# Moving the routing pieces of a sparse-attention and expert kernel ahead of the masks within a step, and releasing its last value loads

## The chip, the cores and the metric

The kernel runs on one core of a Trainium2 chip. The metric is the time of one execution in device microseconds (us). Several executions of each kernel are timed and their median is compared. One further execution is recorded by the hardware profiler; every row below is from that one.

## The reference

Attention over 8 batches and 8 heads of 576 positions with 64 columns, then a layer of experts over the 4608 rows that result. Heads 0 to 3 look at the last 32 positions ("local"), heads 4 to 7 at every 32nd position ("strided").

```python
stride = 32
scores = scale * np.matmul(q, k.transpose(0, 1, 3, 2))
mask_local = (rel >= 0) & (rel < stride)
mask_strided = (rel >= 0) & (pos[None, :] % stride == pos[:, None] % stride)
masks = np.stack([mask_local if h < H // 2 else mask_strided for h in range(H)], axis=0)
scores = np.where(masks[None, :, :, :], scores, -1000000000.0)
attn = np.exp(scores - np.max(scores, axis=-1, keepdims=True))
attn = attn / (np.sum(attn, axis=-1, keepdims=True) + 1e-09)
x = np.matmul(attn, v)                      # then rows (batch, position) of 512 columns
logits = x @ w_gate + modality_bias[modality_id]
e_idx = np.argmax(logits, axis=1)           # one expert of 8 for each row
for e in range(E):
    mask = e_idx == e
    h = np.maximum(x[mask] @ w1[e], 0.0)    # 512 -> 1024
    out[mask] = gate_w[mask, None] * (h @ w2[e])
```

## The kernel before, in words

The work has two stages. The attention stage (about the first 147 us) goes over 32 units, `units`, which alternate between the classes `Local` and `Strided`. Eight units in a row belong to one pair of batches, so there are four pairs, `bp` 0 to 3; unit numbers 7, 15, 23 and 31 end a pair (`ends`). The expert stage then takes 12 blocks of rows, one after the other, each through the two matrices of its expert, in `ffn`.

The attention stage is one loop over steps, `for n in range(nu + 3)`. Several units are in flight in a step. In step n TensorE issues, in the order of the text (`manual_schedule` holds TensorE to it):

1. the scores of unit n (`scores`, L354 for a local unit, L449 for a strided one);
2. in some steps a piece of routing that was flagged as early (`waited`, `pop(1)`);
3. the transposes of the exponents of unit n-2 (`turn`, L224, tiles `t` or `ts`), whose result ScalarE and VectorE copy out (`et` at L378 and L381, `eb` at L484 and L488);
4. the masks of unit n+1 (`masks`, L343 or L442), which open the tiles that its scores are added to;
5. the values of unit n-3 (`values`, L391 and L397, or L499);
6. at the end of the step, transposes of a finished part of the pair (`turn_rows`, tile `xs`, copied at L514) in the two steps behind the end of a pair, and one piece of the work that a finished pair leaves (`pop(1)`).

That work is the generator `after`, which runs `finish_pair` and `route`. For pairs 0 to 2 its pieces come one a step, from step 8bp+10 on: transposes of the rows (tile `xl`, copied at L524), the logits (`lg`, L597 and L602, copied at L605), their transposes (`lt`) with transposes `xs`, more `xs`, the ranks (`rk`, L663 and L664, which read the running counts that L645 writes), and the entries of the lookup table (`en`, L695). The early piece of item 2 is `en`.

All tiles that TensorE writes come from one pool of eight banks of PSUM (`pa`), so a bank has to be emptied by ScalarE or VectorE before it is written again. On the engines other than TensorE a planner orders the instructions that aren't pinned, and it also picks the bank.

Loads are issued from SyncE's queue (SP), in the order of the text. Queries and keys come three steps ahead (`load`, L316 and L419). Values come in two parts each (`load_values`, L324 for a local unit, L424 for a strided one): part 0 of unit n-1 is issued in step n and is held by `after_landing` until TensorE has done the last transpose of unit n-2 (`point`), and part 1 until it has done the last value matmul of unit n-3 (`valued`). Local units take two buffers of `vv` in turn, strided ones two of `vsp`. Stores of finished rows (`store_rows`, L585 on SP for pair 2) stand behind them in the same queue, in the order of the text. From step 27 (`BEGIN`) each step also issues two gathers for the expert stage on GpSimd's queue (POOL); each waits for the last evacuation of the values in front of it (`pace`).

Of the kernel before, what the change touches and what calls it, by code (L numbers as in the profile page):

```python
# [40 lines left out]
SETUP = 6  # L41
POPS, POPF = 5, 3
LT, RS, RK = 7, 9, 11
LAG = 2
PLANE, SEND, SPLIT, TURN = 1, 3, 6, 4
LAST, DRAIN = 6, 4
WHEN = {1: 0, 3: 1, 5: 2, 7: 3}
# [1 line left out]
EARLY, BEGIN, HOLD = 3, 27, 26  # L49
# [142 lines left out]
def attention_moe(ctx: ExitStack, tc: tile.TileContext, a, out):  # L192
# [7 lines left out]
    def pa(name):  # L200
        return ps.tile([P, 512], F32, tag="a", name=name)
# [7 lines left out]
    def keep_busy(n, name):  # L209
        t = pa(name)  # L210
        for _ in range(n):
            nc.tensor.matmul(t, idle[:, 0:P], idle[:], start=True, stop=True)  # L212
# [10 lines left out]
    def turned_to(dst, src):  # L223
        return nc.tensor.transpose(dst, src, ident)  # L224
# [14 lines left out]
    def routing_setup():  # L239

        pin(nc.sync.dma_start(rt[:], a["rt"]))
        pin(nc.sync.dma_start(ld[0:1, :], a["nul"][:, 0:2]))
        pin(nc.sync.dma_start(xd[NT:NT + 1, :].bitcast(I32), a["nul"][:, 2:2 + DM]))
        modf = lp.tile([P, 36], F32, bufs=1, name="modf")
        pin(nc.gpsimd.tensor_copy(modf[:], modi))
        nmod = lp.tile([P, 36], F32, bufs=1, name="nmod")
        pin(nc.gpsimd.tensor_scalar(nmod[:], modf[:], -1.0, 1.0, ALU.mult, ALU.add))
        bias0 = lp.tile([P, 36, E], F32, bufs=1, name="bias0")

        def bc_e(t):  # L250
            return t.unsqueeze(2).to_broadcast([P, 36, E])

        def bc_t(t):
            return t.unsqueeze(1).to_broadcast([P, 36, E])

        pin(nc.gpsimd.tensor_tensor(bias[:], bc_e(modf), bc_t(mb[:, 1, :]), ALU.mult))
        pin(nc.gpsimd.tensor_tensor(bias0[:], bc_e(nmod), bc_t(mb[:, 0, :]), ALU.mult))
        pin(nc.gpsimd.tensor_tensor(bias[:], bias[:], bias0[:], ALU.add))
# [46 lines left out]
    class Local:  # L305
# [62 lines left out]
        def turn(self):  # L368
            n, ex = self.n, self.ex
            self.et = et = ets[0]  # L370
            t1 = pa(f"t1{n}").rearrange("p (g q) -> p g q", g=4)
            for k in range(4):
                turned_to(t1[:, k, :], ex[:, 2 * k:2 * k + 2, :])
            t2 = pa(f"t2{n}")[:, :P]
            self.point = turned_to(t2, ex[:, 9:11, :])
            for par in range(2):
                r = slice(64 * par, 64 * par + 64)
                nc.scalar.copy(et[r, 0:16, par, :], t1[r].rearrange("p k (u q) -> p (k u) q", u=4))  # L378
            for jj in range(2):
                r = slice(64 * jj, 64 * jj + 64)  # L380
                nc.scalar.copy(et[r, 16:18, jj, :], t2[r, 64 * jj:64 * jj + 64].rearrange("p (b q) -> p b q", b=2))  # L381
# [127 lines left out]
    def turn_rows(bp, xt, xcs, c, k0):  # L509
        kn = min(4, 9 - k0)  # L510
        t = pa(f"xs{bp}{c}{k0}").rearrange("p (g q) -> p g q", g=4)
        for k in range(kn):
            turned_to(t[:, k, :], xcs[2 + c][:, P * (k0 + k):P * (k0 + k + 1)])
        nc.scalar.copy(xt[:, k0:k0 + kn, 256 + P * c:256 + P * c + P], t[:, :kn, :])  # L514
# [64 lines left out]
    stores, tabulating = [], []  # L579
# [281 lines left out]
    def after_landing(ins, other):  # L861
        tc.add_manual_dep(ins.ins, other.ins.name, landed, reason="transfers kept apart")
# [90 lines left out]
    def settle(n):  # L953
        while len(late) > n:
            late.pop(0)()
# [55 lines left out]
    def ffn(fp, n, xh, xl, les, between, load=None):  # L1011
# [40 lines left out]
        for f in range(8):  # L1052
# [12 lines left out]
            between(f)  # L1065
            settle(LAG)
        if wide:
# [11 lines left out]
    units, ends = [], {}  # L1079
# [10 lines left out]
    def after(bp, xt, xcs):  # L1090
        yield from finish_pair(bp, xt, xcs)
        if bp >= EARLY:
            yield
            yield from tabulate(bp)
# [10 lines left out]
    def pop(k):  # L1105
        for _ in range(k):
            early.clear()
            while extra:
                got = next(extra[0], extra)
                if got is not extra:  # L1110
                    early.extend([got] if got else ())
                    break
                extra.pop(0)
# [43 lines left out]
    def issue(count):  # L1157
        for _ in range(count):
            if queue and (queue[0][0] >= len(plan) or plan[queue[0][0]][1] in tables):
                queue.pop(0)[1]()  # L1160
# [6 lines left out]
    for what in ORDER.split():  # L1167
        i = int(what[1])
        queue.append((0, partial(load, 0, i)) if what[0] == "w" else (i, partial(begin[what[0]], i)))

    nu = len(units)
# [12 lines left out]
    for n in range(nu + 3):  # L1184
        if n + 3 < nu:
            units[n + 3].load(0)
        if n in FILL:
            keep_busy(FILL[n], f"warm{n}")
        if n < nu:
            units[n].scores()  # L1190
        waited = bool(early)
        if n + 3 < nu:
            after_landing(units[n + 3].load(1), units[n].scored)
        if waited:
            pop(1)
        if 2 <= n <= nu + 1:
            units[n - 2].turn()
        if 1 <= n <= nu:
            ins = units[n - 1].load_values(0)
            if n >= 2:  # L1200
                after_landing(ins, units[n - 2].point)
        if n + 1 < nu:
            units[n + 1].masks()
        if n == nu + 1:
            turn(0)
        if n >= 3:
            units[n - 3].values()
        if 1 <= n <= nu:
            ins = units[n - 1].load_values(1)
            if ins and n >= 3:  # L1210
                after_landing(ins, units[n - 3].valued)
        if n >= 3:
            if n - 3 in ends:
                extra.append(after(*ends[n - 3]))
        if n == SETUP:
            routing_setup()
        if n + 2 < nu:
            units[n + 2].prep()
        ready = len(stores) if n >= HOLD else 9
        if n - 1 in ends or n - 2 in ends:  # L1220
            turn_rows(*ends[n - 1 if n - 1 in ends else n - 2], 0 if n - 1 in ends else 1, 0)
        pop(POPS if n == nu + 2 else 1)
        for _ in range(min(ready, STORED.get(n, SPREAD[(n - 2) % 8]))):
            if stores:
                stores.pop(0)()
        if n >= BEGIN:
            issue(2)
        if n in TABLES:
            for _ in tabulating[-1]:
                break  # L1230
# [6 lines left out]
    for k, (n, *_) in enumerate(plan):  # L1237
        def between(f):
            pop(POPF)
            if TURNED <= k + 1 < len(plan):  # L1240
                if f == PLANE:
                    sent[k + 1] = plane_tokens(plan[k + 1][0], *gathered[k + 1])
                if f == SEND:
                    sent[k + 1] = send_tokens(*sent[k + 1])
                if f == SPLIT:
                    turned[k + 1] = split_tokens(plan[k + 1][0], (k + 1) % 2, *sent[k + 1])
            elif f == TURN:
                turn(k + 1)
            if k + 1 == width and f == LAST:
                turned[width] = turn_last(*gathered[len(plan)], turned[width])  # L1250
            if k == width and f == DRAIN:
                pin(nc.gpsimd.drain())
            issue((2, 1, 1, 1, 2, 1, 2, 1)[f] if k == 0 else f > 1)
# [60 lines left out]
```

## Time and profile before

| | |
|---|---|
| median of 3 runs | 583.21 us |
| lowest and highest of them | 580.5 and 588.86 us |
| the profiled execution | 581.83 us |
| its span, first to last instruction | 580.0 us |
| TensorE busy (modelled ends) | 564.3 us, 97% of the span |
| VectorE, ScalarE, GpSimd busy | 381.7, 325.0 and 197.2 us |

The span lies inside the time of its execution, here 1.83 us shorter. "Busy" is the time in which an engine has an instruction running; a matmul's end is modelled, so TensorE's idle time is read from the list of its waits and from the times between groups. "Issue" as a releaser means that the profile shows nothing that the engine waited for. In the chain of work a group's time is the time until its successor, without the modelled tail.

### The profile page before, as it was taken

The numbers are of one execution on the slowest core, as the hardware profiler recorded it, in microseconds if no ns is written. First come the engines' busy times: TensorE is split into PE (matmuls) and PEld (weight loads), VectorE is DVE, ScalarE is ACT, GpSimd is POOL, SyncE is SP. The second block draws the span as 40 slices with busy tenths as digits, with TensorE's granted clock in tenths as the row PEclk, the third lists the DMA queues.
The fourth block names the chain that finished last, engine by engine and source line by source line (L and its number), as shares of the span: only waits on it lengthen the run. The fifth ranks groups of instructions, "written<-read, shape, count | busy, mean of one in ns | idle before, by whom it ended". The sixth has DMA issues, their size and how long they took to land.

```text
span 580.0 us, 13584 instructions
## 1 busy us (share of the span) xinstructions
PE 564.3 (97%) x5383; PEld 495.1 (85%) x5385; DVE 381.7 (66%) x909; ACT 325.0 (56%) x646; POOL 197.2 (34%) x198
## 2 busy tenths in 40 slices
PE   9999999998999999999999999999999999999995
PEld 5878888877788899989999998989898998998884
DVE  7886977967867874676674757666475666655410
ACT  5789898897744544554454544545363555545312
POOL 3011120125464315444344334554434445320102
PEclk9999999999999999999999999999999999999999
DMA  8988898978985308566543266142414156772102
GB/s 299 332 287 298 287 326 292 327 229 296 313 296 196 118 12 308 187 199 223 154 164 74 61 211 216 47 88 73 90 33 99 52 200 174 262 162 72 56 0 76
DMA packets 62699, 104.28 MB, mean 180 GB/s; under 512 B 36451, under 2 KB 36963, under 8 KB 58532
## 3 DMA queue, kind: packets, MB, share of 16 engines
q0 software_dynamic: 15456, 57.47, 28.6%
q1 hardware_dynamic: 45636, 43.29, 25.5%
q10 hardware_dynamic: 1536, 2.58, 1.4%
q8 instruction: 44, 0.72, 0.5%
q14 instruction: 27, 0.22, 0.1%
HBM read 94.09 MB, written 19.18 MB: 195 GB/s over the span
## 4 chain that ended last, share of the span: by engine, by line
PE 82%; issue 10%; ACT 3%; DVE 2%; POOL 1%; POOLq 0%; ACTq 0%
PE h L1022 31%; PE o L1037 30%; PE s L354 3%; PE ss L449 3%; PE o L391 2%; PE ot L499 2%; PE lg L597 2%; PE xl L224 2%; PE t L224 2%; PE xs L224 1%; PE warm L212 1%; PE ts L224 1%; POOL out L1044 1%; ACT xc L507 1%; PE en L695 1%
## 5 line engine op out<-in xcount | busy, mean ns | idle before, releaser
L1059 DVE TENSOR_TENSOR wl<-raw,wh 128x512 fp32r<-128x512 f32 x176 | 115.2, 692 | 66.8 <-ACT wh L1058 56.7
L1058 ACT CAST wh<-raw 128x512 fp32r<-128x512 f32 x176 | 100.5, 619 | 99.4 <-PE o L1037 81.5
L1022 PE MATMUL h<-xh,wl 128*128 128x384 f32 x352 | 118.7, 337 | 0.0
L1022 PE MATMUL h<-xl,wh 128*128 128x384 f32 x352 | 118.2, 336 | 0.0
L1022 PE MATMUL h<-xh,wh 128*128 128x384 f32 x352 | 117.4, 337 | 0.0
L1037 PE MATMUL o<-wl,hh 128*128 128x512 f32 x264 | 104.1, 394 | 0.0
L1037 PE MATMUL o<-wh,hl 128*128 128x512 f32 x264 | 104.0, 395 | 0.0
L1037 PE MATMUL o<-wh,hh 128*128 128x512 f32 x264 | 103.2, 391 | 0.0
L1025 ACT ACTIVATE hh<-h 128x384 fp32r<-128x384 f32 x88 | 43.2, 491 | 82.4 <-PE h L1022 71.0
L1027 DVE SCALAR_TENSOR_TENSOR hl<-h,hh 128x384 fp32r<-128x384 f32 x88 | 48.9, 555 | 56.5 <-ACT hh L1025 55.1
L921 POOL DMA_INDIRECT raw<-in_w,wi x44 | 51.8, 1177 | 61.3 <-ACT hh L1025 50.8
L1022 PEld LDWEIGHTS h<-xh,wh 128*128 128x128 f32 x352 | 66.2, 188 | 4.2 <-PE xs L224 0.4
L1022 PEld LDWEIGHTS h<-xl,wh 128*128 128x128 f32 x352 | 66.1, 188 | 2.9
L1022 PEld LDWEIGHTS h<-xh,wl 128*128 128x128 f32 x352 | 66.0, 188 | 0.4 <-DVE wl L1059 0.4
L889 POOL DMA_INDIRECT fx<-xd,le x33 | 37.2, 1129 | 76.8 <-ACT wh L1058 42.2
L1037 PEld LDWEIGHTS o<-wh,hl 128*128 128x128 f32 x264 | 49.5, 188 | 10.5
L1037 PEld LDWEIGHTS o<-wl,hh 128*128 128x128 f32 x264 | 49.5, 188 | 8.6
L1037 PEld LDWEIGHTS o<-wh,hh 128*128 128x128 f32 x264 | 49.6, 188 | 8.2
L906 POOL DMA_INDIRECT le<-ld,li x33 | 35.5, 1076 | 41.9 <-DVE li L828 17.6
L1044 POOL DMA_INDIRECT out<-y,le x33 | 34.6, 1049 | 41.3 <-ACT y L1043 37.0
L589 POOL DMA_DIRECT2D xd<-xt x18 | 10.0, 558 | 64.9 <-ACT xc L507 28.2
L983 DVE COPY work<-fx 128x1536 uint16<-128x1536 uint16 x16 | 27.2, 1743 | 0.0
(215 smaller groups left out, 872.6 us busy)
## 6 DMA issues: line engine op xcount, KB each, us to landing
vv<-in_vl SPq DMA_DIRECT2D x32, 292.5 KB
qks<-in_qks SPq DMA_DIRECT2D x32, 288.0 KB
qk<-in_qkl SPq DMA_DIRECT2D x16, 304.0 KB
qk<-in_qkl SPq DMA_DIRECT2D x16, 288.0 KB
xd<-xt POOLq DMA_DIRECT2D x18, 256.0 KB
vsp<-in_vs SPq DMA_DIRECT2D x16, 256.0 KB
xd<-xt SPq DMA_DIRECT2D x9, 256.0 KB
xd<-xt ACTq DMA_DIRECT2D x2, 1024.0 KB
```

What stands on the lines that cost most here:

```text
L224: return nc.tensor.transpose(dst, src, ident)
L889: ins = in_turn(nc.gpsimd.indirect_dma_start(xt[:, h, :], None, xd[0:xrows, :], IOA(ap=le[:, h, 0:1], axis=0), **bounds))
L906: in_turn(nc.gpsimd.indirect_dma_start(le[:, h, :], None, ld[0:1 + last, :], IOA(ap=li[:, s, h:h + 1], axis=0)))
L921: ins = nc.gpsimd.indirect_dma_start(raws[j].rearrange("p f c -> p (f c)"), None, a["w"], IOA(ap=wi[:, s, j:j + 1], axis=0), bounds_check= ...
L983: pin(nc.vector.tensor_copy(rows[:, :, w, :], halves(xt)[:, :, :, w]))
L1022: nc.tensor.matmul(hp, w[:, a1], x[:, c, 0:size], start=(k == 0), stop=(k == 11))
L1025: steps.append(nc.scalar.activation(hh[:, 0:size], hp, AF.Relu))
L1027: nc.vector.scalar_tensor_tensor(hl[:, 0:size], hp, 0.0, hh[:, 0:size].bitcast(F32), ALU.max, ALU.subtract)
L1037: nc.tensor.matmul(os[h], hx[:, m], w[:, 512:1024], start=(f == 0 and i == 0), stop=(f == 7 and i == 2))
L1044: outs.add(in_turn(nc.gpsimd.indirect_dma_start(out, IOA(ap=le[:, i, 0:1], axis=0), y[:], None, bounds_check=NT - 1, oob_is_err=False), True))
L1058: nc.scalar.copy(wh[:, c], raw[:, c])
L1059: nc.vector.tensor_tensor(wl[:, c], raw[:, c], wh[:, c].bitcast(F32), ALU.subtract)
```

## The change

It has two parts. First, `turn_rows` and the pair's piece `pop(1)` no longer stand at the end of a step but right behind `turn` of unit n-2, in front of the value load, the masks and the values. In the step in which a pair's generator is appended (n-3 in `ends`) and in the last step, the piece stays at the end. Second, the value loads of units 28 to 31 are no longer held by `after_landing`; unit 28's are issued in step 29 as before, those of units 29 and 30 both in step 30, and unit 31's in step 31, so units 30 and 31 come a step sooner in the text.

```diff
-LAG = 2
+LAG, FREE = 2, 29
...
         if 2 <= n <= nu + 1:
             units[n - 2].turn()
-        if 1 <= n <= nu:
+        ready = len(stores) if n >= HOLD else 9
+        if n - 1 in ends or n - 2 in ends:
+            turn_rows(*ends[n - 1 if n - 1 in ends else n - 2], 0 if n - 1 in ends else 1, 0)
+        beside = n <= nu + 1 and n - 3 not in ends
+        if beside:
+            pop(1)
+        if 1 <= n < FREE:
             ins = units[n - 1].load_values(0)
             if n >= 2:
                 after_landing(ins, units[n - 2].point)
+        for i in {FREE: (FREE - 1,), FREE + 1: (FREE, FREE + 1), FREE + 2: (FREE + 2,)}.get(n, ()):
+            for part in range(2):
+                units[i].load_values(part)
         if n + 1 < nu:
             units[n + 1].masks()
         if n == nu + 1:
             turn(0)
         if n >= 3:
             units[n - 3].values()
-        if 1 <= n <= nu:
+        if 1 <= n < FREE:
             ins = units[n - 1].load_values(1)
             if ins and n >= 3:
                 after_landing(ins, units[n - 3].valued)
...
-        ready = len(stores) if n >= HOLD else 9
-        if n - 1 in ends or n - 2 in ends:
-            turn_rows(*ends[n - 1 if n - 1 in ends else n - 2], 0 if n - 1 in ends else 1, 0)
-        pop(POPS if n == nu + 2 else 1)
+        if not beside:
+            pop(POPS if n == nu + 2 else 1)
         for _ in range(min(ready, STORED.get(n, SPREAD[(n - 2) % 8]))):
```

## Rows read from the trace of the kernel before

**Rows 1.** Windows: length, busy PE, PEld, DVE, ACT, POOL; clock, DMA share, GB/s.

```profile
0.00:120.00 120.00, 114.78 (x2697) 95.85 (x2700) 98.72 (x354) 99.79 (x226) 18.84 (x37) 1.00 0.91 304
120.00:147.00 27.00, 23.14 (x473) 18.93 (x474) 18.49 (x69) 22.25 (x54) 12.78 (x13) 1.00 0.80 272
147.00:573.00 426.00, 426.00 (x2216) 380.30 (x2215) 264.52 (x487) 202.28 (x367) 163.62 (x147) 1.00 0.45 140
```

**Rows 2.** Waits of PE, 0 to 165 us: total, times, longest.

```profile
PE s L354 <- issue: 2.2, 2, 1.1
PE ss L449 <- issue: 1.2, 2, 0.9
PE o L391 <- issue: 1.2, 3, 0.4
...
PE o L391 <- ACT xt L514: 0.6, 2, 0.3
PE ts L224 <- DVE pbf L676: 0.6, 1, 0.6
PE ot L499 <- ACT eb L488: 0.6, 1, 0.6
```

**Rows 3.** Chain of work, step 20: start, time, what.

```profile
85.10 1.15 PE ot L499 x32
86.25 1.86 PE lg L597 x32
```

**Rows 4.** Timeline of PE, step 15: start, time, instruction, idle before and releaser.

```profile
63.33 0.41 PE L343 MATMUL s<-cb_sb 128*128 128x256 bf16 x2
...
64.79 0.69 PE L391 MATMUL o<-vv,et 128*64 128x65 f32 x16 [0.32 <-ACT xt L514]
```

**Rows 5.** Timeline of all engines, lines of ACT, steps 14 and 15.

```profile
59.59 1.18 ACT L378 COPY et<-t 64x512 f32<-64x512 f32 x2 [0.88 <-PE t L224]
...
64.17 0.73 ACT L514 COPY xt<-xs 128x512 f32<-128x512 f32 x2
```

**Rows 6.** Timeline of ACT, step 19: the copies of the row transposes.

```profile
83.73 1.41 ACT L524 COPY xc<-xl 128x512 f32<-128x512 f32 x4
```

**Rows 7.** Timeline of DVE, 96 to 99 us: the running counts of pair 1.

```profile
97.48 0.31 DVE L645 TENSOR_TENSOR_SCAN cum<-ohb 128x72 bf16<-128x72 bf16 x1
```

**Rows 8.** Timeline of PE, steps 23, 32 and 33.

```profile
100.17 0.21 PE L663 MATMUL rk<-ohb,cb_sb 128*128 128x72 bf16 x1
...
139.45 1.22 PE L499 MATMUL ot<-eb,vsp 104*64 104x72 f32 x32 [0.62 <-ACT eb L488]
140.60 0.66 PE L224 MATMUL xs<-cf_sb,xc 128*128 128x128 f32 x4
141.88 0.61 PE L224 MATMUL ts<-cf_sb,enp 128*96 128x128 f32 x4 [0.62 <-DVE pbf L676]
...
146.87 0.49 PE L224 MATMUL xs<-cf_sb,xc 128*128 128x128 f32 x3 [0.86 <-issue]
```

**Rows 9.** Timeline of DVE, steps 31 and 32.

```profile
137.00 0.46 DVE L461 TENSOR_REDUCE mxs<-ss 128x16 f32<-128x288 f32 x1 [1.84 <-PE o L397]
...
141.27 0.46 DVE L470 TENSOR_TENSOR enp<-exs,sms 128x288 f32<-128x288 f32 x1
```

**Rows 10.** Timeline of SP's queue: the value loads of units 30 and 31.

```profile
137.71 0.80 SPq L324 DMA_DIRECT2D vv<-in_vl  x2
...
139.08 1.94 SPq L424 DMA_DIRECT2D vsp<-in_vs  x2
```

**Rows 11.** Windows of 2 and 1 us, columns as in Rows 1.

```profile
126.00:128.00 2.00, 2.00 (x57) 1.72 (x57) 1.30 (x3) 1.55 (x5) 1.01 (x1) 1.00 0.05 9
...
143.00:144.00 1.00, 1.00 (x16) 0.83 (x16) 0.95 (x2) 1.00 (x3) 0.70 (x2) 1.00 1.04 397
```

**Rows 12.** The page, DMA queue of instructions: packets, MB, share.

```profile
q8 instruction: 44, 0.72, 0.5%
```

**Rows 13.** The page, DMA issues: value loads of local units, two a unit, KB each.

```profile
vv<-in_vl SPq DMA_DIRECT2D x32, 292.5 KB
```

## The prediction, made before the changed kernel had run

> **What bounds the kernel now.** I read the windows by stage first. From 147 to 573 us TensorE has no idle time at all, and its granted clock is 1.00, the 2.4 GHz level [rows 1]. The change touches nothing there, so that stage can only begin earlier or later. In front of it TensorE is idle for 120 - 114.78 = 5.22 us up to 120 us, and for 27 - 23.14 = 3.86 us up to 147 us, 9.1 us together [rows 1]. TensorE is thus the bound of the attention stage too, though the DMA engines are busy for 0.91 of its first 120 us and VectorE and ScalarE for over 0.8. A step can be shortened only by idle time of TensorE; the matmuls are the same before and after.
>
> The list of TensorE's waits says what the idle time is [rows 2]. There are 2.2 + 1.2 + 1.2 us in scores and values with no releaser ("issue"), and one more of 0.86 us inside four transposes of old data [rows 8]: 5.5 us in which the engine, by the profile, waited for nothing. The waits that have a releaser are two of 0.6 us in all for a copy of `xs`, one of 0.6 us for `eb`, and one of 0.6 us for VectorE in front of the last transposes of exponents: 1.8 us. The remaining 1.8 us of the 9.1 lie in the start and in pieces too small to name. No wait of TensorE is for a value load: neither `vv` nor `vsp` stands there as a releaser.
>
> So the change has 1.8 us of named waits to work on, 5.5 us of nameless ones, and the stalls that it may add.
>
> **The pieces.** What moves costs TensorE nothing by itself: the largest piece, `lg`, takes 1.86 us in the chain behind values of 1.15 us [rows 3], and in the new order the two change places, with the next scores starting when they did. 23 steps are touched: 8 with `turn_rows` and 5 a pair for the pieces of pairs 0 to 2 (the sixth and later pieces issue no matmul, or are flagged early). I go through what could wait in the new place.
>
> *Inputs of the pieces.* They come from the piece a step before, whose place moves up as well, so the distance is kept. If the other engines' products don't move up with it at all, the margins are these: the copies of `xl` in pair 1 end at 83.73 + 1.41 = 85.14 [rows 6]; `lg` would begin at 85.1 instead of 86.25 [rows 3], and its first half (0.9 us) reads tiles that were done steps ago, so it has about 0.8 us. The running counts of pair 1 end at 97.48 + 0.31 = 97.79 [rows 7]; `rk` began at 100.17 [rows 8], and without the values (about as long as a strided unit's 1.15 us), the masks and the wait in front of it this becomes about 98.4. Both margins are thin but positive. Cost 0, with 0.4 us a pair at worst.
>
> *Banks.* In step 15 of pair 0 values stand still until a copy of `xs` has emptied a bank: the matmul starts at 64.79 after 0.32 us [rows 4], and the copies run from 64.17 [rows 5]. The list has two such waits [rows 2], so one a pair for pairs 0 and 1. Behind it is ScalarE, which has no idle time between the copies at 59.59 and those at 64.17 [rows 5]: `xs` is done long before, its copy has no turn. Moving the transposes up by the masks and values in front of them (about 1.3 us) therefore does not bring the copy forward unless the planner also places it ahead. I take 0; the bounds are -0.6 us (both waits go) and, if the masks of that step, now at 63.33 [rows 4], must have that bank, 64.79 - 63.33 = 1.46 us in place of 0.32, which is +1.1 us a pair and +3.4 us for three.
>
> *The end of the stage.* In step 32 the values of unit 29 wait 0.62 us for `eb`; then come four `xs`, and the transposes of unit 31 wait 0.62 us for VectorE [rows 8]. In the new order `xs` (0.6 us) stands in front of the values and covers the first wait. But the second is then longer by what the first gave: the normalised exponents end at 141.27 + 0.46 = 141.73 [rows 9] whatever TensorE does in between. What could bring them forward is `rk`, which moves in front of the values of unit 28: VectorE stands idle 1.84 us up to 137.00 [rows 9], and the short instructions of the piece now lie between the two rows in its queue. If they slip into that idle time, up to the whole wait of 0.6 us is saved; if the queue keeps its order, nothing. I take -0.3 us, half; bounds 0 and -1.2 us (both waits).
>
> **The value loads.** SP issues the loads of units 30 and 31 at 137.71 and 139.08 [rows 10]. Unit 30's are 2 x 292.5 = 585 KB [rows 13], 2.2 us at the 272 GB/s of this stretch [rows 1], unit 31's of like size. Unheld, they move up to where the queue gets to them, some 6 us earlier; unit 28's move into a lull (DMA share 0.05 at 126 to 128 us, against 1.04 at 143 to 144 us [rows 11]). The values of unit 31 are wanted behind 146.87, so no wait for data ends sooner. In SP's queue the stores of pair 2 stand behind the loads and are passed by none that waits longer. What is left is indirect: of the nameless waits, 1.2 us in values and 0.86 us in `xs` lie between 136 and 147 us [rows 2, 8], where the DMA engines are full. If these are instructions that arrive late (44 packets and 0.72 MB go over a queue of their own [rows 12]), less traffic there may shorten them. Since no row shows a fetch beside a gap, and traffic is moved here and not saved, I take half of the 2.1 us, -1.0 us; bounds -2.1 us, and +1.0 us if the gaps merely move to where the traffic now is.
>
> The Trainium skill, "Runtime: NRT & Kernel Launch", section "Instruction fetch mechanics", says that a sequencer fetches its instructions in blocks of 16 KiB over its own DMA queue and that this is mostly hidden. The size agrees: 0.72 MB in 44 packets are 16.4 KB each [rows 12]. By "mostly hidden" the 1.0 us would be 0 and the sum -0.3 us. Against the change speaks "DMA: Bandwidth & Descriptors", section "Issuing engines are not separate DMA queues": transfers issued from SP, ScalarE and GpSimd share the same 16 engines and interleave. By it three value loads in a row would slow the gathers and fetches that run beside them, and the sum would be +0.7 us: -0.3 us and the upper bound of +1.0 us.
>
> **Sum.** 0 (pieces) + 0 (banks) - 0.3 (end of the stage) - 1.0 (gaps) = -1.3 us. The profiled execution took 581.83 us, 1.83 over its span of 580.0; the sum gives it 580.5 us. Its time lies 1.38 us below the median of the three runs. With all four executions (580.5, 581.83, 583.21, 588.86) the middle is 582.5, and the forecast is 582.5 - 1.3 = 581.2 us.
>
> **Rivals.** *Nothing moves.* The planner and the shared queues give back what the order takes, and the gaps stay where the instruction stream puts them: 582.5 us. For it speaks that 5.5 of the 7.3 us are nameless, and that the waits at the end hang on VectorE.
>
> *All waits go.* Both `xs` waits (-0.6), both waits at the end (-1.2) and the gaps between 136 and 147 us (-2.1): 582.5 - 3.9 = 578.6 us. It needs the planner to put the copies of the moved pieces first on ScalarE. Against it: ScalarE is full in exactly those steps.
>
> *A wait for a bank in front of the masks.* The pieces take one to four banks of eight and now take them ahead of the masks and values of the same step. Where ScalarE has a backlog, TensorE stands at the masks until the piece's copy is done, and the scores of the next step stand behind it in order. The price is the +3.4 us above for the step with three `xs` tiles a pair; the step with four `xl` tiles, whose copies ScalarE reaches late too [rows 6], adds the same once more if it goes alike: up to 6.8 us. With the first alone 582.5 + 3.4 = 585.9 us, with both 589.3. It decides from the point at which the piece's copy comes later than the masks' turn, which the rows show for step 15 by 1.5 us. Against it: the same tiles needed the same banks within a step before, and the wait was 0.3 us. To lose 2% (11.7 us) each of the 23 moved steps would have to lose 0.5 us.
>
> **How the numbers follow.** Forecast 0.42, nothing moves 0.23, all waits go 0.13, the bank wait 0.22 (its larger form 0.05). The range runs from the fastest case less the scatter of a median (the lowest run is 2 us under the middle), 576, to between the two forms of the bank wait, 587.5. Less than 2% is about what a measurement of this kernel can't tell from no change; that is 571.5 to 594.9 us. Faster than that would need more idle time than TensorE has in this stage: 0.02. Slower would need the bank wait in most of the steps: 0.04. Within: 0.94.
>
> **What would show it.** Right: the stretch from 147 us on has the same length, and the list of waits of TensorE is short by about 1 us, its nameless waits behind 136 us the shorter ones. The values of unit 29 have no wait for `eb`, and the last `ts` still waits for VectorE. The SP queue issues unit 30's and 31's loads before 135 us. For the bank rival: waits at L343 or L442 with a copy at L514 or L524 as releaser. The prediction is wrong if the order of ScalarE's or VectorE's queue changes so far that TensorE waits in steps that have no piece, or if a piece waits for its own input.

## The result and the profile after

The changed kernel takes 585.37 us (median of 15 runs, 584.29 to 588.47), the kernel before, timed beside it, 582.31 us (15 runs): a ratio of 1.006, 95% interval 1.0043 to 1.0077, so 2.5 to 4.5 us slower. The time is inside the range of the prediction (576 to 587.5) and on the other side of its forecast (581.2). The ratio, like those below, is estimated from the executions in the faster of two states of the chip, and so isn't the quotient of the two medians (1.0053). The profiled execution has a span of 582.5 us against 580.0.

The windows of the changed kernel, columns as in [rows 1]:

```profile
0.00:120.00 120.00, 109.67 (x2624) 92.78 (x2626) 96.40 (x340) 97.23 (x221) 18.85 (x37) 1.00 0.90 298
120.00:147.00 27.00, 23.32 (x518) 20.01 (x518) 19.92 (x82) 22.58 (x53) 10.82 (x11) 1.00 0.85 275
147.00:573.00 426.00, 424.53 (x2237) 378.98 (x2234) 264.62 (x489) 202.73 (x371) 161.69 (x148) 1.00 0.45 141
```

TensorE stands idle for 10.33 us up to 120 us, where it stood for 5.22 [rows 1]; up to 147 us it is 14.0 us in place of 9.1. From 147 us on 1.5 us of idle time are new. The clock is 1.00 in all three, so in these two executions none of this is the clock.

TensorE's waits up to 165 us, answering to [rows 2] (total, times, longest; a line with "..." stands for rows left out):

```profile
PE o L391 <- issue: 3.2, 3, 1.8
PE ss L449 <- issue: 2.4, 4, 1.0
PE s L354 <- issue: 1.9, 3, 0.9
PE ts L224 <- DVE enp L470: 1.3, 1, 1.3
...
PE ot L499 <- issue: 1.1, 3, 0.4
PE ot L499 <- DMA vsp<-in_vs: 0.6, 1, 0.6
PE ts L224 <- issue: 0.4, 1, 0.4
PE o L391 <- ACT xc L524: 0.4, 2, 0.2
PE s L343 <- ACT xc L524: 0.4, 2, 0.2
```

Three readings. The named waits that the change aimed past are gone: neither `xs` (L514) nor `eb` (L488) stands in the list, the rows left out included. In their place are the wait of the last `ts`, twice as long (1.3 for 0.6 us), and small ones for copies of `xl` (L524), two of them in front of the local masks. The 0.6 us for a value load (`vsp`) lie at 19.36 us, 13 us ahead of the first moved piece (32.69 us), where both kernels issue the same matmuls: so much differs between two executions without the change. And what grew most has no releaser: in scores and values the "issue" waits were 2.2 + 1.2 + 1.2 = 4.6 us [rows 2] and are now 3.2 + 2.4 + 1.9 + 1.1 = 8.6.

The wait counts miss half of the story. The same stretch as a chain of work (start, time, what), first the kernel before, with `lg` between values and scores:

```profile
46.60 0.47 PE o L391 x16
47.06 1.24 PE xl L224 x10
48.31 1.20 PE s L354 x36
...
50.32 1.15 PE ot L499 x32
51.47 1.86 PE lg L597 x32
53.34 0.22 PE lg L602 x8
53.56 1.23 PE ss L449 x64
...
68.81 0.59 PE xs L224 x4
```

then the changed kernel:

```profile
48.34 0.47 PE o L391 x16
48.81 1.05 PE s L354 x36
...
50.55 1.86 PE lg L597 x32
52.42 0.22 PE lg L602 x8
52.63 0.23 PE ss L442
52.86 1.15 PE ot L499 x32
54.02 1.11 PE ss L449 x64
...
67.60 0.44 PE xs L224 x4
```

The same 36 scores take 1.05 us in place of 1.20 where they stand right behind values, the 64 strided ones 1.11 in place of 1.23. Four `xs` transposes of step 16 behind those of exponents take 0.44 us, where they took 0.59 between values and scores. A moved piece of four transposes thus gives TensorE back some 0.3 us, in two places. The logits (`lg`) take 1.86 us in either place.

To put both sides into one sum I took the start times of all matmuls from the first scores to the first matmul of the experts. Where two starts lie over 250 ns apart, all but 60 ns is counted as a stop (except beside the filling matmuls on idle data near the start), the rest of the stretch as work. A stop is a "block" stop if it lies within 6 matmuls of a whole multiple of 125.4, counted from matmul 470 (472 in traces that have two more of the filling matmuls on record), and the matmul behind it starts within 1.7 us of the end of a 16.4 KB packet of instructions (all explained below). "Rest" is from there to the last matmul:

```
                      stage   work   stops: block  other    rest
before                144.7  134.3          3.6     6.9    421.9
after                 145.9  128.0          8.3     9.7    423.3
```

So the change took 6.3 us of work away from TensorE, got 4.7 us of block stops and 2.8 us of other stops for it, and lost 1.4 us at the start of the experts: -6.3 + 4.7 + 2.8 + 1.4 = +2.6 us, to the rounding the difference of the spans. Of the growth of the other stops, 0.7 us are the last `ts`; some 1.7 us of them stand around `xl` (below), and 0.8 us are the one at 19.36 us, which the change can't have made. The 60 ns are a rough allowance: with the usual distance of each pair of neighbours in its place, the work fell by 4.7 us and the stops rose by 5.8, and the sum is the same.

**What the nameless stops are.** One of them, in the timeline of TensorE (start, time, what, idle before):

```profile
71.26 0.41 PE L343 MATMUL s<-cb_sb 128*128 128x256 bf16 x2
71.60 0.56 PE L391 MATMUL o<-vv,et 128*64 128x65 f32 x11
74.01 0.39 PE L391 MATMUL o<-vv,et 128*64 128x65 f32 x5 [1.85 <-issue]
```

It comes in the middle of 16 equal matmuls that wait for the same things: no semaphore explains it. Numbered from the start, the matmuls behind such stops are 470, 595, 845, 970, 1222, 1598, 2226, 2351, 2603: whole multiples of 125.4 apart to within a few matmuls, in both kernels (the kernel before has 470, 846, 2606). 125.4 matmuls with their weight loads are 251 instructions, and the profile's queue of instructions has 44 packets of 16.4 KB [rows 12], for 5383 matmuls and 5385 weight loads. Read from the trace, packet by packet, for the three block stops of the kernel before and the six longest of the changed one (us; a stop is counted from start to start, so it is some 0.2 us longer than the idle time in the timeline; the last column is from the packet's end to the next matmul):

```
         packet          matmul   its start   stop   end to start
before   22.45  23.39      470      24.73     1.35      1.34
         37.93  38.97      846      40.25     1.34      1.28
        112.94 113.91     2606     115.32     1.07      1.41
after    22.56  23.64      470      25.04     1.09      1.40
         37.71  38.67      845      40.04     1.05      1.37
         55.43  56.31     1222      57.66     0.69      1.35
         71.48  72.59     1598      74.01     2.07      1.42
         99.44 100.38     2226     101.77     1.15      1.40
        114.56 116.64     2603     117.93     1.20      1.29
```

TensorE stands until some 1.4 us after a packet of its own instructions has landed. Where the packet had ended 2 us or more before the matmul at the boundary, one boundary of the two kernels shows a stop of over 0.25 us (0.67 in the changed one). A packet starts 1.8 us on the mean after TensorE passes the boundary before it in the kernel before, 2.4 us in the changed one, single ones at 4.0 and 4.5 us; its transfer takes about 1 us. Together with the 1.4 us that is 4.2 us on the mean before, and up to 6.9 us, and a block of 125.4 matmuls lasts 5.5 us on the mean. The stage has little room to spare here.

### The profile page after: what moved, and what is told of

It is laid out like the page before. It is cut to its first block, busy times and chain, and to the rows that moved or that the text cites. A ratio compares the mean times of both kernels' runs of the same rounds, so it can differ in the third digit from the quotient of the medians.

```text
span 582.5 us, 13580 instructions
## 1 busy us (share of the span) xinstructions
PE 560.5 (96%) x5383; PEld 493.8 (85%) x5385; DVE 380.9 (65%) x909; ACT 324.6 (56%) x646; POOL 195.1 (33%) x198
## 4 chain that ended last, share of the span: by engine, by line
PE 77%; issue 11%; DVE 3%; ACT 3%; DMA 3%; POOL 1%; POOLq 0%; SPq 0%; ACTq 0%; DVEq 0%
PE h L1022 30%; PE o L1037 30%; PE o L391 3%; PE ot L499 3%; PE ss L449 2%; PE s L354 2%; DMA vsp<-in_vs 1%; DMA raw<-in_w,wi 1%; PE t L224 1%; PE ts L224 1%; PE lg L597 1%; POOL out L1044 1%; PE warm L212 1%; PE xs L224 1%; ACT wh L1058 1%
## 5 line engine op out<-in xcount | busy, mean ns | idle before, releaser
L889 POOL DMA_INDIRECT fx<-xd,le x33 | 35.0, 1061 | 76.9 <-ACT wh L1058 24.9
```

The costliest lines, as they stand in the source:

```text
L889: ins = in_turn(nc.gpsimd.indirect_dma_start(xt[:, h, :], None, xd[0:xrows, :], IOA(ap=le[:, h, 0:1], axis=0), **bounds))
```

## The experiments

All times are medians, ratios against the kernel before timed beside the same runs, each with a 95% interval. The kernel before took 582.11 us beside the first four runs, 580.25 beside the four on the loads, 580.32 beside the two with fewer loads, the shifted and the padded change, and 580.03 beside the last four. Sums by stage come from one profiled execution of each kernel, and stages of kernels with the same order differ by some us. In the cuts of code, "..." stands for lines left out.

### Which part of the change

Theories: A, the end of the stage (the last `ts`) costs the time; B, the moves in the steps before it; C, the unheld loads.

**Pieces moved, loads held as before:** the diff without its FREE lines.

> All pieces moved as in the change, value loads held as before. The change as a whole measured about +3 us (ratio 1.006). Theory A (end of the stage: values of steps 26 to 34 come later, so gathers, weights and ScalarE's queue run late): about +3 us. Theory B (TensorE's own work gets shorter, but its instruction blocks then arrive too late, all along the stage): about +3 us. Theory C (the unheld value loads disturb other transfers): within 1 us of the kernel before.

585.95 us, 1.006 (1.004 to 1.008): all of the loss.

**Loads unheld, nothing moved:** the FREE lines alone.

> Only the value loads of units 28 to 31 are unheld; all pieces stay at the end of their step. Theories A and B: within 1 us of the kernel before. Theory C: about +3 us.

583.18 us, 1.0019 (0.9994 to 1.0044): no change that can be told, and C falls as the main cause. The gain of 1.0 us that I had given these loads isn't there either: block stops are 4.6 us, before 3.6.

**Moved in steps before 26 alone, loads held:**

```
+        rows_first = n < 26
+        if rows_first and (n - 1 in ends or n - 2 in ends):
...
+        beside = n <= nu + 1 and n - 3 not in ends and n < 26
```

> Pieces and row transposes moved in steps before 26 alone (pairs 0 and 1, 15 of the 23 places), loads held as before. Theory A: within 1 us of the kernel before, since nothing at the end moves. Theory B: about +2 us, two thirds of the whole. Theory C: 0.

586.07 us, 1.0083 (1.005 to 1.0116): by the middle values the whole loss or more.

**Moved from step 26 on alone, loads held** (the same with `n >= 26`):

> Pieces and row transposes moved in steps from 26 on alone (pair 2 and the last rows), loads held as before. Theory A: about +3 us. Theory B: about +1 us. Theory C: 0. If A holds, the transposes of the logits of pair 3 wait for ScalarE again (about 1.2 us), as in the changed kernel.

582.74 us, 1.0004 (0.9977 to 1.0031). The last `ts` waits 1.4 us here, as in the changed kernel (1.3), and no loss can be told; the wait of the first `lt` for ScalarE isn't there (rest 422.0). A falls, B stands: the loss comes from the steady part of the stage, where no wait had been named.

### Are the blocks late because the loads are bunched?

In the new order the second half of a unit's values and the next unit's loads are released close together. Theory D: the bunch delays the packets; E: TensorE, faster in the new order, gets to the boundary too early.

**The old order, with the releases spaced as in the new one:**

```
+        if 4 <= n <= 31:
+            after_landing(units[n - 2].load_values(1), units[n].began)
+        if n + 3 < nu and n >= 4:
+            units[n + 3].load(0)
...
+        if 1 <= n <= nu and not 3 <= n <= 30:
             ins = units[n - 1].load_values(1)
```

This spaces the loads so in all steps, not in the moved ones alone.

> TensorE's order of the kernel before, but the second half of a value load, and the first half of the queries' load behind it, are released only when the next unit's scores begin, as far behind the transposes and as close in front of the next load as in the changed kernel. Theory D (the move brings three loads closer together; TensorE's instruction blocks, which travel on the same DMA engines, then come late): 3 to 5 us slower than before, nameless waits of TensorE up from about 5.5 us towards 10 us with its own work unchanged (about 134 us between first scores and first expert matmul). Theory E (the blocks come late because TensorE itself runs through them faster in the new order): within 1 us of before.

581.09 us, 1.002 (0.9998 to 1.0042); block stops 3.3 us, work 133.5.

**The change, second half of the values held until the masks of the next unit:**

```
+        if 1 <= n < FREE:
+            ins = units[n - 1].load_values(1)
+            if n >= 3:
+                after_landing(ins, units[n + 1].opened)
```

> The changed kernel, but the second half of a value load is held until the masks instead of the last value matmul, so that loads are spread over the step again. Theory D: nameless waits back to about 5 to 6 us while TensorE's work stays short (about 128 to 130 us), so 3 us faster than the kernel before, 6 us faster than the change. Theory E: as slow as the change, about 3 us over the kernel before.

582.70 us, 1.0041 (1.0014 to 1.0069); block stops 11.9 us, work 128.3.

**The kernel before, no value load held:** both `after_landing` lines of the value loads taken out.

> The kernel before without any hold on value loads: they are issued as soon as the queue and the buffers allow, so more transfers are under way at once. Theory D: slower than before by 2 us or more, nameless waits above 8 us. Theory E: within 1 us, since TensorE's order is the old one.

579.99 us, 1.0001 (0.9976 to 1.0026); block stops 4.8 us, work 133.8.

**The change, first half of the values held until the masks:** as above, with `load_values(0)`.

> The changed kernel, but the first half of a value load is held until the masks, behind the piece, and the second as in the change. The loads of a step are then apart by about the times of the kernel before, with the piece between the queries' second half and the values' first. Theory D: nameless waits below 7 us, 1 to 3 us faster than the kernel before. Theory E: as slow as the change.

581.27 us, 1.0022 (0.9996 to 1.0048); block stops 6.8 us, work 127.4.

In block stops and work the four split by order, not by spacing: the old order has 3 to 5 us of block stops whatever its loads do, the new one 7 to 12. D falls as the main cause of the block stops. In time they don't split: the old order with the new spacing and the change with the first half at the masks both stand at 1.002, with intervals that hold 1. Where the loads are released shifts the size of the stops within an order (6.8 to 11.9), and by the middle values some two thirds of the change's loss, so it plays a part. In the last run half of what the stage gained in the profile (141.0 us against 144.7) is lost again behind it (rest 423.7 against 421.9).

### Less traffic, shifted boundaries, padding

For E against F (the stops belong to the order by something else than the fetch).

**The change with fewer loads, and the kernel before with fewer loads:**

```
+            self.vv = vvs[n % 2]
+            if n >= 2:
+                return None
```

(the same in the strided units, which keep the values of unit 0 or 1).

> The change, but the value loads are left out from unit 2 on in either kind (each unit multiplies by the values of unit 0 or 1, so the output is not the reference's): 14 MB less traffic in the stage. Theory E (TensorE's instructions come in blocks of 256 over the same DMA engines as the data; a block's packet begins 2.4 us on the mean after TensorE reached the block before it, and can be used 1.4 us after it ends, so that an order in which TensorE is through a block sooner stands at the next one): packets begin within 1.5 us, stops at block boundaries fall from 8.4 us to under 3, the work stays at 128 us, and the stage is 3 to 6 us shorter than that of the old order with the same loads left out. Theory F (the stops belong to the order, by where the boundaries fall in its steps or by a wait that the profile doesn't name): stops stay at 6 us or more, and this kernel stays 2 to 4 us slower than the old order with the same loads left out.

> The kernel before with the same value loads left out. E: it has only 1.3 us of stops at boundaries to lose, its work stays at 134 us, so that it gains little and is 3 to 6 us slower than the change with the same loads left out. F: 2 to 4 us faster than that.

637.1 us and 636.07 us, 1.0982 (1.093 to 1.1034) and 1.0963 (1.0914 to 1.1012). With other values the tokens are routed otherwise: the experts do 180 matmuls more and take some 58 us more in both, so only the stages are compared: 141.3 us (work 126.8, block stops 1.7, other 12.8) and 139.5 us (work 132.5, block 2.1, other 4.9). The DMA share of the first 120 us is down to 0.71 in both. E's first half came true: beyond the one at matmul 472 no block stop is left, in either order, and packets start 1.5 us behind their boundary. Its second half failed: the new order isn't 3 to 6 us shorter, but 1.8 us longer. What took the place of the block stops is in TensorE's waits of the change with fewer loads (line numbers are shifted in this file: L345 is L343, L356 is L354, L503 is L499, L528 is L524):

```profile
PE s L345 <- ACT xc L528: 2.7, 5, 1.0
PE s L356 <- issue: 1.5, 1, 1.5
...
PE ot L503 <- DVE ex L366: 1.3, 3, 0.5
```

and in its timeline:

```profile
77.88 1.39 PE L224 MATMUL xl<-cf_sb,xt 128*128 128x128 f32 x10
80.24 0.27 PE L345 MATMUL s<-cb_sb 128*128 128x256 bf16 x1 [0.97 <-ACT xc L528]
80.73 0.30 PE L345 MATMUL s<-cb_sb 128*128 128x320 bf16 x1 [0.22 <-ACT xc L528]
81.22 0.69 PE L393 MATMUL o<-vv,et 128*64 128x65 f32 x16 [0.20 <-ACT xc L528]
```

This is the wait for a bank in front of the masks: the piece with four `xl` tiles takes four banks, and masks and values get them one by one as ScalarE copies each out, 1.4 us in this pair. The changed kernel has the same place with 0.16, 0.22 and 0.20 us:

```profile
83.03 0.27 PE L343 MATMUL s<-cb_sb 128*128 128x256 bf16 x1 [0.16 <-ACT xc L524]
83.52 0.30 PE L343 MATMUL s<-cb_sb 128*128 128x320 bf16 x1 [0.22 <-ACT xc L524]
84.01 0.69 PE L391 MATMUL o<-vv,et 128*64 128x65 f32 x16 [0.20 <-ACT xc L524]
```

There TensorE had stood for 2.1 us at a block boundary 9 us before, time in which ScalarE could catch up; that this is why the waits are smaller is argued, not shown.

**The change, boundaries shifted by half a block:**

```
-            keep_busy(FILL[n], f"warm{n}")
+            for _ in range(8 * FILL[n] - (n - 2) * 8):
+                nc.tensor.matmul(t[0:32, 0:64], idle[:, 0:32], idle[:, 0:64], start=True, stop=True)
```

> The change with 62 matmuls more ahead of the stage's steps 2 and 3 (ten long matmuls of idle data become 72 short ones of about the same time): every block boundary moves by half a block against the steps. E: stops of 6 to 10 us at the new boundaries, time that of the change within 1.5 us. F by place of the boundaries: the stops change by more than 3 us, and the time with them.

586.86 us, 1.0114 (1.0062 to 1.0166): 3 us over the change's ratio of 1.006, though the intervals overlap. Block stops are 13.2 us. They lie again at multiples of 125.4 matmuls, 348, 724, 848, 1476 and on, though every step now stands 62 matmuls later: they follow the blocks, not the steps, which is E's. Their size depends on where in a step a boundary falls, which is F's, and by the numbers set down before the run F's came true: the stops grew by more than 3 us, and the time with them. One of the stops, 3.8 us at 41.85 us, is in doubt: the packet ended 1.3 us before it, but the profile names a copy by ScalarE (`qz`, ended at 41.79 us) as its releaser. Without it the block stops are 9.4 us. Both theories hold a part.

**The change with padding:**

```
+                for _ in range(2 if 4 <= self.step <= 25 else 1):
+                    nc.tensor.matmul(s, identb, cb[:, M_L + 64 * g0:M_L + 64 * (g0 + gn)], start=True, stop=True)
...
```

> The change with the mask matmuls of units 4 to 25 issued twice (33 matmuls, about 4 us of TensorE's time, same result). E: TensorE gets later to its block boundaries and stands there less, by 2 to 4 us; the time is that of the change within 1.5 us. F, or TensorE being the bound with its stops unavoidable: 3 to 4 us slower than the change.

582.2 us, 1.0044 (1.002 to 1.0069), for the change's 1.006: 33 matmuls more, and nothing lost that could be measured. The sum shows where they went, though for the slowest of its twelve executions (585.6 us), the one that was profiled: work 134.1 us in place of 128.0, block stops 4.2 in place of 8.3, stage 146.4 in place of 145.9. In the waits two stops at block boundaries are left (L451 is L449, L355 is L354), beside a bank wait (L344 is L343):

```profile
PE ss L451 <- issue: 2.2, 1, 2.2
PE s L355 <- issue: 1.5, 2, 1.3
...
PE s L344 <- ACT xc L526: 1.0, 1, 1.0
```

Only 3.7 us of the added work is the padding (by the next run). The rest is a second price of a block stop, seen in its windows (columns as in [rows 1], the clock third from the end):

```profile
26.00:28.00 2.00, 2.00 (x58) 1.75 (x58) 1.97 (x8) 1.51 (x4) 0.00 (x0) 1.00 0.84 252
28.00:31.00 3.00, 0.93 (x52) 0.83 (x46) 1.16 (x3) 2.90 (x7) 0.00 (x0) 0.92 0.81 283
31.00:34.00 3.00, 2.85 (x22) 2.11 (x24) 1.58 (x3) 0.69 (x3) 1.35 (x5) 0.50 0.73 201
34.00:37.00 3.00, 3.00 (x62) 3.00 (x60) 1.92 (x9) 1.21 (x3) 1.30 (x2) 0.50 0.50 136
37.00:40.00 3.00, 3.00 (x63) 2.66 (x62) 2.88 (x8) 1.74 (x5) 0.00 (x0) 0.95 0.85 282
```

TensorE stood for 2.2 us from 28.9 us on, and its clock fell to 0.50, the 1.2 GHz level, for 6.8 us. Falls of 3.4 or 6.8 us within the stage are in six of the eighteen profiled executions: with the pieces moved (all of them, early ones alone, shifted, padded, without the `xl` piece) and once in the old order (`BEGIN` 26). Four of them follow a block stop of 2.3 to 3.8 us, two a row of stops of half a microsecond; but stops of 2.6 us at the boundary near matmul 1599 passed without a fall in two kernels. The profiled executions of the changed kernel and of the kernel before have no fall in the stage. The mean granted clock of every timed execution is on record, over its whole length: with the pieces moved alone it is under 0.996 in six of nine, in the kernel before beside it in eight of 28. But the other three have a median of 585.28 us and the other twenty one of 581.94: 3.3 us apart. So a lower clock was more frequent in the new order, and the loss is there without it.

**The kernel before with the same padding:**

> The kernel before with the mask matmuls of units 4 to 25 issued twice (33 matmuls, about 4 us of TensorE's time, same result). Theory E (instruction blocks come late where TensorE is fast, so the padding is free in the new order): the old order has only 1.3 us of stops at block boundaries, so it shows most of the padding, +2 to +4 us. Rival (TensorE's work is not the bound of the stage in either order): within 1 us of before, as in the padded change.

581.38 us, 1.0033 (1.0008 to 1.0057), +1.9 us (0.5 to 3.3) for 3.7 us of work more (138.0 for 134.3). That is at the lower edge of E's 2 to 4 and more than nothing, but the interval doesn't rule out the rival's 1 us: the old order seems to have had some idle time to absorb padding in. That the new one has more is not shown by these two intervals. (The 1.3 us of block stops in this expectation, and in that of the kernel before with fewer loads, are 3.6 by the rule of the table.)

### The bank wait by itself, and two attempts to win

**The change, the piece with four xl tiles left where it was:**

```
-        beside = n <= nu + 1 and n - 3 not in ends
+        beside = n <= nu + 1 and n - 3 not in ends and n - 4 not in ends
```

> The change, but the piece with four xl tiles (one step of each pair) stays behind the values, as before. If the bank wait in front of the masks is a part of the loss, the waits at the local masks for a copy of xc go (three pairs, about 1 us each), and the time is 1 to 3 us under the change's (582.3 to 584.5 beside a before of 582). If block stops are all of the loss: as the change, ratio 1.005 or more.

580.72 us, 1.0033 (1.0001 to 1.0065): half of the change's loss is left by the middle values, with intervals that overlap. The waits at the local masks are gone; block stops are 6.2 us. Its chain shows the work term, too: with the piece back in its place `xl` takes 1.24 us and the scores behind it 1.20, as before, while those behind values elsewhere keep their 1.05:

```profile
83.92 0.47 PE o L391 x16
84.39 1.24 PE xl L224 x10
85.63 1.20 PE s L354 x36
```

**The same, with the first half of the values at the masks, and the experts' loads begun a step sooner** (`BEGIN` 26 for 27):

> The change with the xl piece unmoved, the first half of the value loads held until the masks, and the expert stage's first loads and gathers begun a step sooner (26 for 27). If what the stage gained in the run with the value loads at the masks was given back in front of the first weights: 2 to 3 us under before. If not: within 1.5 us of before.

580.43 us, 1.0014 (0.9987 to 1.0041): with all three, no loss can be told any more, and the interval lies below the change's (1.0043 to 1.0077).

**The kernel before without holds, and the same `BEGIN`:**

> The kernel before without holds on its value loads (no change in time alone, its stage 3.4 us shorter in the profile and the rest 1.4 longer), and the expert stage's first loads and gathers begun a step sooner. If the rest's delay hangs on when the weights are asked for: 1.5 to 3 us under before. If not: within 1 us of before.

580.6 us, 1.0012 (0.9982 to 1.0041). Neither beats the kernel before, and their rest is no shorter for asking sooner (424.2 and 422.8 us). What costs the rest 1.4 us in some kernels was not tried further. In the changed kernel it is this, ScalarE first, then TensorE:

```profile
162.95 1.14 ACT L1058 CAST wh<-raw 128x512 fp32r<-128x512 f32 x2 [3.98 <-DMA raw<-in_w,wi]
```

```profile
165.95 0.55 PE L224 MATMUL lt<-cf_sb,ls 128*128 128x128 f32 x3 [1.16 <-ACT ls L605]
```

ScalarE's queue stands 3.98 us at a cast for the experts' weights, the copy of `ls` stands behind it, and TensorE gets to `lt` before that copy.

## Why the prediction was wrong

**"The matmuls are the same before and after", "What moves costs TensorE nothing by itself".** This step failed first. The matmuls are the same, their time isn't: work fell by 4.7 to 6.3 us, by how a stop is counted. The price of a matmul was read from rows where it stood in the old order; the rows of steps without a piece, in the same trace, had the scores at 1.05 us already (16.88 us into the trace of before). By itself it should have made the kernel faster.

**The gaps, -1.0 us.** The term that decided. The guess that these are instructions that arrive late was right: block stops, shown by the packets, by the shift and by the runs with less traffic. Its sign and size were wrong. I gave the change a gain for traffic moved out of the last steps, and nothing for the stops along the rest of the stage; the loads alone measured +1.1 us, with an interval that holds zero and not -1.0. I never asked what a faster TensorE does to a fetch that runs one block ahead, and block stops rose by 4.7 us. Two readings under this term were wrong too: unit 31's loads are 288 KB, about half of unit 30's 585, and unheld they were issued at 137.38 us, 1.7 us sooner and not some 6 (unit 30's at 132.01, 5.7 us sooner). The "mostly hidden" of the Trainium skill ("Runtime: NRT & Kernel Launch", "Instruction fetch mechanics") fits the kernel before, where three of some 25 block boundaries of the stage show a stop (3.6 us together), better than the changed one, where nine do (8.3 us). Such a stop can also cost clock, as the padded run shows; the executions at a granted clock of 0.996 and more show the loss without that.

**Inputs of the pieces, 0.** Right: no wait of TensorE in the moved pieces is for their inputs; `rk` of pair 0 ran at 64.34 us without one.

**Banks, 0.** The two waits for `xs` went (-0.6, the lower bound). The rival's wait came, in front of the masks as it said, but in the step with four `xl` tiles and not in that with three `xs`, and with 0.4 us at masks and 0.4 at values in place of 3.4 and more. With fewer loads, and so without block stops, it was 2.7 us at the masks alone. The run without that move has about half of the loss. That the measured 585.37 us lies beside this rival's 585.9 is in good part luck: its waits are a quarter of the 3.4 us that it was priced at.

**End of the stage, -0.3 us.** Both waits as forecast: the one for `eb` gone, the last `ts` waiting for VectorE, longer by what the first gave. VectorE's normalised exponents ended later than before (144.41 us for 141.73), and the 0.3 us weren't won; the moves from step 26 on measure 1.0004 (0.9977 to 1.0031).

**147 us on, unchanged.** Not quite: 1.4 us were lost, 1.16 of them in the wait of the first `lt`. The kernel before without holds shows such a loss too (rest 423.3), and the pieces moved alone don't (422.0), at the same ratio as the change; so it is neither bound to this order nor needed for the loss.

**What stays open.** Why packets start later in the new order (2.4 us behind the boundary for 1.8) was not settled: the DMA engines are 0.9 busy in both, less traffic brings it to 1.5 in both, and spacing and place of the boundaries each move it. How the loss divides between block stops and bank waits isn't fixed either, because taking away the block stops made the bank waits grow; in the sum of the profiled pair the stops of both kinds take back the whole gain in work and 1.2 us more. What decides the 1.4 us in front of the experts is open, too, and so is how much of the 585.37 us is owed to the lower clock of eleven of its fifteen executions.

## What to carry to other kernels

Before costing a reorder at nothing, read the time of the same group of matmuls behind different neighbours in the trace; and before counting that as a gain, look what else is due at that pace. Nameless stops at a fixed distance in instructions are blocks of the engine's own code, fetched by the same busy DMA engines: the faster order met more of them here, and padding it cost nothing that could be measured. When several limits lie within a few per cent of each other, taking one away shows the next, so the test is a run in which the first is gone.

## What the runs showed of the hardware

- In this kernel the instructions of TensorE come in packets of 16.4 KB, one for every 125.4 matmuls with their weight loads. Each starts once the boundary of the block before is passed (1.8 and 2.4 us behind it on the mean), takes about 1 us, and where TensorE had to stand for it, it went on 1.3 to 1.4 us after its end. At a DMA share of 0.9 single packets started over 4 us behind the boundary; at 0.71 no block stop was left but the one at matmul 472.
- The time of a group depends on the group in front of it: 36 scores took 1.20 us behind transposes and 1.05 behind values, 4 transposes 0.59 us behind values and 0.44 behind transposes.
- 3.7 us of added matmuls cost 1.9 us (0.5 to 3.3) in the old order, and in the new one nothing that could be measured.
- Stops of TensorE of 2.3 to 3.8 us were followed by a fall of its granted clock to 0.50, the 1.2 GHz level, for 3.4 or 6.8 us in four executions; stops of 2.6 us were not in two others.
